# Row flags in one word, the overflow path as one loop, and expert 0's rest without branches

## The chip, the cores and the metric

The kernel runs as one program on one core of a Trainium2 chip. The metric is the device time of one execution in microseconds. Five engines work beside each other, each with its own queue of instructions: TensorE (PE; its weight loads are shown apart as PEld), VectorE (DVE), ScalarE (ACT), GpSimd (POOL) and SyncE (SP). They wait for each other on semaphores. In front of each engine a sequencer takes the program in order: it executes branches, register loads and register arithmetic itself and hands the rest on to the engine. In the profile the sequencers' own rows carry a q (PEldq, SPq, POOLq).

## The reference, cut to what matters

Three stages follow one another: a linear attention, a dense feed-forward layer with a cosine gate, and a layer of 8 experts, of which each token uses one. The change lies between the last two.

```python
logits = x @ w_gate                      # x: 3072 tokens x 384
e_idx = np.argmax(logits, axis=1)
...
for e in range(8):
    mask = e_idx == e
    h = np.maximum(x[mask] @ w1[e], 0.0)     # 384 x 1024
    ye = h @ w2[e]                           # 1024 x 384
    out[mask] = gate_w[mask, None] * eom[mask, e, None] * ye
```

## The kernel before

Attention and the dense layer run interleaved over six groups of 512 tokens. Each token's row is then written by a POOL scatter into the region of its expert in the array `xs`, at a place found by counting (`route_rank`, `route_rows`; `base` holds for each expert its first free row). Each expert has `CAP` = 448 rows that are always computed; what lies above them is done by an overflow path, entered only if an expert has more rows.

An expert's work has two stages. Stage 1 (`e_stage1`) makes the hidden layer in 8 blocks of 128 units (j = 0 to 7): 9 matmuls each, three exact splits times three slices of 128 input dimensions, all rows of the expert at once as columns of one PSUM bank `hp`. ACT then writes the high part of relu(hp), DVE the low part, and only then may PE reuse the bank. Stage 2 (`e_part2`) multiplies each tile of 128 rows of the hidden layer with `w2`; the last, half tile of 64 rows has a form of its own (`e_part2_both`). While one expert runs, the next expert's weights are loaded in 8 pieces through four buffers `raw` (SP), split into a high part (ACT, line 595) and a low part (DVE, line 599), and its rows `xe` are loaded and transposed (`load_rows`, `rows_trans`).

If an expert has at most `LOW` = 384 rows, its `few` flag is set: stage 1 then takes 384 columns instead of 448, and the half tile is left out. Both forms stand in the program, and PE's sequencer branches between them (`by_rows`): once for each of the 8 blocks and once for the half tile, for each expert.

Expert 0 is special. Its first 256 rows (`early`) are done while the dense layer's last group still runs (`first`, `second`); its remaining 192 rows (128 where `few` is set) come after, with the same weights. In the run shown they have 192 columns.

The order on PE, ACT, DVE and SP around this seam is the order in which the code is written (a manual schedule up to the last `second`, program order behind). At the seam the kernel before does this: transposes of expert 0's remaining rows, `second(7)`, start of the load of expert 1's rows, then on DVE the overflow counts `nt` and the flags `few` (lines 1017 to 1030), then on PE a load of 8 flags from SBUF into 8 registers (line 1031), then on DVE the zeroing of three PSUM banks (line 1037), then stage 1 of expert 0's remaining rows on two banks, in turn. In the trace the 8 flags are one TENSOR_LOAD and, for each flag, a FUSED_REGOPS and a SEQ_ASSERT. `ps_m` is a PSUM pool of three banks that the transposes use; at this point of the program it is otherwise free.

At the end every engine loads `nov`, the largest overflow count, and branches around the overflow path, which is written out for 8 experts. In this run it is not entered.

Of the kernel before, what the change touches and what calls it, by code (L numbers as in the profile page):

```python
# [28 lines left out]
E = 8  # L29
# [5 lines left out]
CAP = 448  # L35
# [15 lines left out]
CEB = CW8 + GU * E  # L51
CTOK = CEB + E
CROW = CTOK + NU
CCOL = CROW + 1


@with_exitstack
def kernel(
# [590 lines left out]
    def by_rows(few, sizes):  # L649

        if few is None:
            yield sizes[0]
            return
        with tc.If(few > 0) as cmp:  # L654
            yield sizes[1]
        with cmp.Else():
            yield sizes[0]

    def e_stage1(r, j, hh, hl):
        h1, l1 = ew[r["e"]][:2]  # L660
        xh, xl = r["x"]
        n = r["n"]
        hp = (r["banks"][j % 2] if "banks" in r else ps_h.tile([128, 512], F32, tag="h", name="hp"))[:, :n]
        fs = slice(j * 128, (j + 1) * 128)
        m_n = n - CAP + LOW
        few = r.get("few")
        for m in by_rows(few, (n, m_n)):
            i = 0
            for w, x in ((h1, xh), (h1, xl), (l1, xh)):
                for k in range(KD):  # L670
                    nc.tensor.matmul(  # L671
                        out=hp[:, :m], lhsT=w[:, k, fs], rhs=x[:, k, :m], start=(i == 0), stop=(i == 3 * KD - 1)
                    )
                    i += 1
        nc.scalar.activation(out=hh, in_=hp, func=ACTF.Relu)  # L675
        for c, out_ in hl:
            nc.vector.scalar_tensor_tensor(  # L677
                out=out_, in0=hp[:, c], scalar=0.0, in1=hh[:, c].bitcast(F32), op0=ALU.max, op1=ALU.subtract
            )
        r["h"][j] = (hh, hl[0][1])  # L680
# [264 lines left out]
    with tc.manual_schedule(engines={ENG.PE, ENG.Activation, ENG.DVE, ENG.SP}):  # L945
# [7 lines left out]
        def second(j):  # L953
            for t in range(n_t):
                e_part2(early, t, accs[t], j)
# [22 lines left out]
            x1_rows(g, s)  # L978
        route_rank(g)
        route_rows(g)  # L980
        for s in range(GU):
            route_send(g, s)
        second(1)
# [7 lines left out]
        second(5)  # L991
        first(7)
        second(6)
        m1.close()

        m2 = ExitStack()
# [5 lines left out]
        def begin(e):  # L1002
            r0 = EARLY if e == 0 else 0
            return load_rows(e, r0, CAP - r0, z_p, "xe")
# [4 lines left out]
        for t in range(n_t):  # L1009
# [2 lines left out]


        nt = o_p.tile([128, E + 1], F32, name="nt")
        few = o_p.tile([128, E], F32, name="few", bufs=1)
        fewi = o_p.tile([128, E], U32, name="fewi", bufs=1)
        nc.vector.tensor_tensor(out=nt[:, 0:E], in0=base, in1=ebase, op=ALU.subtract)
        nc.vector.tensor_scalar(
            out=nt[:, 0:E], in0=nt[:, 0:E], scalar1=float(127 - CAP), scalar2=127.0, op0=ALU.add, op1=ALU.max
        )  # L1020
        nc.vector.tensor_reduce(out=nt[:, E:E + 1], in_=nt[:, 0:E], axis=AX.X, op=ALU.max)

        nc.vector.tensor_scalar(
            out=few, in0=base, scalar1=float(LOW), scalar2=None, op0=ALU.subtract
        )
        nc.vector.tensor_tensor(out=few, in0=few, in1=ebase, op=ALU.is_le)
        nc.vector.tensor_copy(ntl, nt)
        nc.vector.tensor_scalar(out=ntl, in0=ntl, scalar1=7, scalar2=None, op0=ALU.logical_shift_right)

        nc.vector.tensor_copy(fewi, few)  # L1030
        few_r = nc.values_load_multi_w_load_instructions(fewi[0:1, 0:E], engines=[ENG.PE], min_val=0, max_val=1)[1]


        banks = [ps_h.tile([128, 512], F32, tag="h", name="hp") for _ in range(2)]
# [2 lines left out]
            nc.vector.memset(b, 0.0)  # L1037

        for e in range(E):
            r["few"], r["banks"] = few_r[e], banks  # L1040
            steps = load_expert(e + 1, vr_p if e % 2 else vl_p) if nxt else []

            def step():
# [37 lines left out]
                e_out(r, t, op, ot)  # L1081
            r = nxt
            nxt = begin(e + 2) if e + 2 < E else None
    m2.close()
    at2.close()


    nov = nc.values_load(ntl[0:1, E:E + 1], min_val=0, max_val=NOV)
    with tc.If(nov > 0):
        with tc.tile_pool(name="ov_p", bufs=1, side="left") as ov_p:  # L1090
            f1 = ov_p.tile([128, KD, EF], F32, name="f1")
            f2 = ov_p.tile([128, NEF, DM], F32, name="f2")
            rid = ov_p.tile([128, 1], F32, name="rid")
            lim = ov_p.tile([128, 1], F32, name="lim")
            far = ov_p.tile([128, 1], F32, name="far")
            ri = ov_p.tile([128, 1], U32, name="ri")
# [4 lines left out]
            oo = ov_p.tile([128, DM], F32, name="oo")  # L1101
            nc.vector.memset(zo, 0.0)
            nc.vector.memset(zo[:, ROW - 1:ROW], float(NT))
            for e in range(E):
                nc.sync.dma_start(out=f1, in_=w1[e].rearrange("(k p) f -> p k f", p=128))
                nc.sync.dma_start(out=f2, in_=w2[e].rearrange("(k p) f -> p k f", p=128))
                r0 = e * REG + CAP
                nc.vector.tensor_scalar_add(rid, c_sb[:, CROW:CROW + 1], float(r0))
                nc.vector.tensor_copy(lim, base[:, e:e + 1])
                n_e = nc.values_load(ntl[0:1, e:e + 1], min_val=0, max_val=NOV)  # L1110
                with tc.For_i(0, n_e, 1) as it:

                    nc.vector.tensor_tensor(out=far, in0=rid, in1=lim, op=ALU.is_lt)
                    nc.vector.scalar_tensor_tensor(
# [5 lines left out]
                        out=xs, out_offset=bass.IndirectOffsetOnAxis(ap=ri, axis=0),  # L1120
                        in_=zo, in_offset=None, bounds_check=E * REG - 1, oob_is_err=False,
                    )
                    nc.sync.dma_start(out=xo[:, 0, :], in_=xs[bass.ds(it * 128 + r0, 128), :])
                    gt, tk = gates(ov_p, xo[:, :, DM:], 1)
                    tp = ps_m.tile([128, KD, C], F32, tag="m", name="tp")
                    for k in range(KD):
# [28 lines left out]
def _layout(inputs):  # L1155
# [32 lines left out]
    for n in range(NU):  # L1188
        c[:, CTOK + n] = (n % B) * S + (n // B) * C + perm
    c[:, CROW] = np.arange(128)  # L1190
    return {
        "units": u.reshape(NU, 128, UCOL),
        "cst": c,
# [26 lines left out]
```

## Time and profile before

| | |
|---|---|
| three timed runs | 814.5 us median, 813.9 to 815.12 |
| the profiled execution | 812.32 us, span 810.5 us, mean granted PE clock 0.981 |
| busy share of the span | PE 95%, DVE 62%, ACT 52%, POOL 39% |
| last transfer into `out` issued at | 800.13 us of the span |

A position in the span is given in us from its start, and so are all times of single instructions. "Granted clock" is the share of 2.4 GHz that TensorE was given; 0.50 is 1.2 GHz. In a row of the timeline the first number is the start, the second the length, "x3" the number of merged instructions, and the bracket tells how long the engine sat idle before and what ended it. The seam lies at 566 to 596 us: in the page's 40 slices PE's tenths are 9 nearly throughout from 140 us on, with one break there.

### The profile page before, as it was taken

How to read it: one execution, taken by the hardware profiler on the slowest of the kernel's cores; microseconds unless marked ns; L12 is line 12 of the kernel's file. 1: busy time of each engine (PE TensorE's matmuls, PEld its weight loads, DVE VectorE, ACT ScalarE, POOL GpSimd, SP SyncE). 2: the span in 40 equal slices, each digit the busy share in tenths (PEclk: the TensorE clock that was granted, in tenths of full speed). 3: DMA queues.
4: the chain of work that ended last, by engine and by line, in shares of the span. 5: the costliest groups of instructions: out<-in, count | busy, mean ns of one | idle time of the engine just before them, and what ended most of it. 6: DMA issues, size and time to landing. Idle time of an engine off the chain costs nothing.

```text
span 810.5 us, 13963 instructions
## 1 busy us (share of the span) xinstructions
PE 769.4 (95%) x5346; PEld 655.7 (81%) x5346; DVE 501.9 (62%) x955; ACT 425.3 (52%) x782; POOL 316.6 (39%) x304
## 2 busy tenths in 40 slices
PE   8679899999999999999999999999699999999994
PEld 5557777888888888888888888889699999999994
DVE  8999998675467537663676334744565655655530
ACT  2454565754575457644665467555354545554420
POOL 3566756544355335543464424662011101101101
PEclk9998999999999999999999999999899999999998
DMA  9524452713201230113010101211565445645201
GB/s 326 205 94 159 170 199 100 243 60 112 80 1 54 73 125 1 54 59 109 31 55 20 41 0 59 89 50 44 182 192 181 135 142 176 191 123 159 67 13 34
DMA packets 46881, 85.31 MB, mean 105 GB/s; under 512 B 4152, under 2 KB 38488, under 8 KB 44240
## 3 DMA queue, kind: packets, MB, share of 16 engines
q1 hardware_dynamic: 43344, 74.67, 28.1%
q0 software_dynamic: 3456, 9.57, 3.2%
q8 instruction: 50, 0.82, 0.4%
q14 instruction: 31, 0.25, 0.1%
HBM read 69.01 MB, written 15.99 MB: 105 GB/s over the span
## 4 chain that ended last, share of the span: by engine, by line
PE 52%; issue 27%; DVE 11%; POOL 4%; DMA 2%; ACT 1%; POOLq 0%; SPq 0%; ACTq 0%; DVEq 0%
PE acc L418 22%; PE hp L379 21%; POOL out_dram L711 4%; DVE cv L347 3%; PE sc L211 2%; DMA un<-in_units_dram 2%; DVE cv L352 2%; PE yp L269 2%; PE yp L261 2%; DVE cv L356 2%; PE pp L285 1%; PE tp L442 1%; DVE t L397 1%; DVE t L392 1%; DVE w L151 1%
## 5 line engine op out<-in xcount | busy, mean ns | idle before, releaser
L405 POOL TENSOR_TENSOR gl<-t,gh 128x512 fp32r<-128x512 f32 x95 | 127.8, 1345 | 182.2 <-ACT gh L404 152.5
L386 ACT ACTIVATE t<-hp 128x512 f32<-128x512 f32 x96 | 57.3, 596 | 140.1 <-PE hp L379 130.4
L397 DVE TENSOR_TENSOR t<-hp,t 128x512 f32<-128x512 f32 x96 | 65.7, 684 | 89.3 <-ACT t L394 89.3
L392 DVE SCALAR_TENSOR_TENSOR t<-t,hp 128x512 f32<-128x512 f32 x96 | 65.7, 684 | 79.7 <-ACT t L386 79.6
L711 POOL DMA_INDIRECT out_dram<-ot,tk x32 | 31.3, 979 | 205.9 <-ACT ot L710 205.6
L687 PE MATMUL op<-h,hb 128*128 128x384 f32 x384 | 102.4, 338 | 1.7 <-PEq L654 1.7
L418 PE MATMUL acc<-gh,woh 128*128 128x512 f32 x288 | 90.3, 421 | 0.0
L677 DVE SCALAR_TENSOR_TENSOR hb<-hp,hb 128x64 fp32r<-128x64 f32 (+3 forms) x136 | 45.3, 372 | 70.1 <-ACT hb L675 70.0
L379 PE MATMUL hp<-xh,wih 128*128 128x512 f32 x288 | 83.6, 398 | 3.7 <-DVE t L397 3.1
L418 PE MATMUL acc<-gl,woh 128*128 128x512 f32 x288 | 84.2, 399 | 0.0
L418 PE MATMUL acc<-gh,wol 128*128 128x512 f32 x288 | 83.9, 399 | 0.0
L379 PE MATMUL hp<-xh,wil 128*128 128x512 f32 x288 | 82.6, 395 | 0.0
L379 PE MATMUL hp<-xl,wih 128*128 128x512 f32 x288 | 82.5, 395 | 0.0
L393 ACT ACTIVATE t<-t 128x512 f32<-128x512 f32 x96 | 60.7, 632 | 38.3 <-DVE t L392 38.3
L675 ACT ACTIVATE hb<-hp 128x448 fp32r<-128x448 f32 (+2 forms) x72 | 36.3, 504 | 72.3 <-PE hp L671 70.3
L599 DVE TENSOR_TENSOR l<-raw,h 128x768 fp32r<-128x768 f32 x60 | 57.3, 957 | 25.8 <-ACT h L595 25.0
L687 PEld LDWEIGHTS op<-h,hb 128*128 128x128 f32 x384 | 69.7, 188 | 3.0 <-issue 3.0
L394 ACT ACTIVATE t<-t,halfpi 128x512 f32<-128x512 f32 x96 | 69.6, 725 | 3.1
L379 PEld LDWEIGHTS hp<-xh,wih 128*128 128x128 f32 x288 | 54.4, 191 | 18.0 <-DVE t L397 2.2
L418 PEld LDWEIGHTS acc<-gh,wol 128*128 128x128 f32 x288 | 55.1, 191 | 13.4
L418 PEld LDWEIGHTS acc<-gl,woh 128*128 128x128 f32 x288 | 54.9, 191 | 12.8
L379 PEld LDWEIGHTS hp<-xl,wih 128*128 128x128 f32 x288 | 54.5, 189 | 12.9
(144 smaller groups left out, 1454.4 us busy)
## 6 DMA issues: line engine op xcount, KB each, us to landing
raw<-in_w_dram SPq DMA_DIRECT2D x64, 384.0 KB, 3.4
un<-in_units_dram SPq DMA_DIRECT2D x20, 1032.0 KB, 4.9
raw<-in_w_in_dram SPq DMA_DIRECT2D x16, 384.0 KB, 3.7
raw<-in_w_out_dram SPq DMA_DIRECT2D x16, 384.0 KB, 4.1
xs<-zrow SPq DMA_DIRECT2D x8, 591.0 KB, 5.8
xe<-xs SPq DMA_DIRECT2D x7, 591.0 KB, 5.1
un<-in_units_dram SPq DMA_DIRECT2D x4, 512.0 KB, 6.2
un<-in_units_dram SPq DMA_DIRECT2D x4, 256.0 KB, 6.8
```

The lines of the kernel that those rows point to most:

```text
L379: nc.tensor.matmul(out=hp, lhsT=w[:, k, fs], rhs=x[:, k, :], start=(n == 0), stop=(n == 3 * KD - 1))
L386: nc.scalar.activation(out=t, in_=hps[g, j], func=ACTF.Copy, bias=MAGIC)
L392: nc.vector.scalar_tensor_tensor(out=t, in0=t, scalar=MAGIC, in1=hp, op0=ALU.subtract, op1=ALU.subtract)
L393: nc.scalar.activation(out=t, in_=t, func=ACTF.Abs)
L394: nc.scalar.activation(out=t, in_=t, func=ACTF.Sin, scale=-TWO_PI, bias=halfpi)
L397: nc.vector.tensor_tensor(out=t, in0=hps.pop((g, j)), in1=t, op=ALU.mult)
L405: eng.tensor_tensor(out=gl, in0=gf, in1=gh.bitcast(F32), op=ALU.subtract)
L418: nc.tensor.matmul(out=acc[g][k], lhsT=w[:, j, ks], rhs=a, start=(j == 0 and n == 0), stop=(j == NF - 1 and n == 2),)
L599: (nc.vector.tensor_tensor if i < 4 else sub)(out=lo, in0=raws[i], in1=h.bitcast(F32), op=ALU.subtract)
L677: nc.vector.scalar_tensor_tensor(out=out_, in0=hp[:, c], scalar=0.0, in1=hh[:, c].bitcast(F32), op0=ALU.max, op1=ALU.subtract)
L687: nc.tensor.matmul(out=op, lhsT=a[:, sl], rhs=w[:, j, :], start=(j == 0 and i == 0), stop=(j == NEF - 1 and i == 2))
L711: sent = nc.gpsimd.indirect_dma_start(out=out, out_offset=bass.IndirectOffsetOnAxis(ap=tk[0:n, t, :], axis=0), in_=ot[0:n], in_offset=None ...
```

## The change

Three edits come together.

1. The flags become bits of one word. Right after the last `route_rows`, DVE computes for each expert whether its count is at most 384, times 2 to the power of the expert's number (a new row of constants), sums the 8 values and converts the sum (four small instructions). PE loads that one word before the transposes of expert 0's remaining rows. Each branch of experts 0 to 7 then tests a bit, with register arithmetic ahead of it. The three DVE instructions and the load of 8 registers at the seam go.
2. Stage 1 of expert 0's remaining rows always takes all 192 columns, with no branch, and goes over three banks in turn: the two of before and one from `ps_m`.
3. The overflow path becomes one loop over the experts instead of 8 copies, and `nov` is loaded before expert 7 instead of at the end.

```diff
-        hp = (r["banks"][j % 2] if "banks" in r else ps_h.tile([128, 512], F32, tag="h", name="hp"))[:, :n]
+        hp = (r["banks"][j % 3 if r["e"] == 0 else j % 2] if "banks" in r and (j % 3 < 2 or r["e"] > 0) else ps_m.tile(
+            [128, 512], F32, tag="m", name="hp") if "banks" in r else ps_h.tile([128, 512], F32, tag="h", name="hp"))[:, :n]
...
-        for m in by_rows(few, (n, m_n)):
+        for m in by_rows(few if r["e"] else None, (n, m_n)):
...
         route_rows(g)
+        cnt = s_p.tile([128, E], F32, tag="rk", name="cnt")
+        nc.vector.tensor_tensor(out=cnt, in0=base, in1=ebase, op=ALU.subtract)
+        nc.vector.scalar_tensor_tensor(
+            out=cnt, in0=cnt, scalar=float(LOW), in1=c_sb[:, CPW:CPW + E], op0=ALU.is_le, op1=ALU.mult
+        )
+        bits = s_p.tile([128, 1], F32, tag="pf", name="bits")
+        nc.vector.tensor_reduce(out=bits, in_=cnt, axis=AX.X, op=ALU.add)
+        fews = s_p.tile([128, 1], U32, tag="pu", name="fews")
+        nc.vector.tensor_copy(fews, bits)
         for s in range(GU):
             route_send(g, s)
...
         second(6)
+        few = nc.values_load(fews[0:1, 0:1], engines=[ENG.PE], min_val=0, max_val=(1 << E) - 1)
...
-        nc.vector.tensor_scalar(
-            out=few, in0=base, scalar1=float(LOW), scalar2=None, op0=ALU.subtract
-        )
-        nc.vector.tensor_tensor(out=few, in0=few, in1=ebase, op=ALU.is_le)
...
-        nc.vector.tensor_copy(fewi, few)
-        few_r = nc.values_load_multi_w_load_instructions(fewi[0:1, 0:E], engines=[ENG.PE], min_val=0, max_val=1)[1]
...
-            r["few"], r["banks"] = few_r[e], banks
+            r["few"], r["banks"] = nc.tensor.snap((few >> e) & 1), banks
...
+            if e == E - 2:
+                nov = nc.values_load(ntl[0:1, E:E + 1], min_val=0, max_val=NOV)
...
-    nov = nc.values_load(ntl[0:1, E:E + 1], min_val=0, max_val=NOV)
-    with tc.If(nov > 0):
+    with tc.If(nov > 0, label="ov"):
...
-            for e in range(E):
-                nc.sync.dma_start(out=f1, in_=w1[e].rearrange("(k p) f -> p k f", p=128))
-                nc.sync.dma_start(out=f2, in_=w2[e].rearrange("(k p) f -> p k f", p=128))
...
+            with tc.For_i(0, E, 1) as e:
+                nc.sync.dma_start(out=f1, in_=w1[bass.ds(e, 1)].rearrange("o (k p) f -> p (o k) f", p=128))
+                nc.sync.dma_start(out=f2, in_=w2[bass.ds(e, 1)].rearrange("o (k p) f -> p (o k) f", p=128))
```

How the seam's instructions stand in the program, for PE and DVE. In PE's order before, from the last matmul of `second(7)` (`op`) over the load of the flags to the first block of stage 1 in its two forms (`hp_5980` is the first bank, `exh`, `exl` the rows, `h1`, `l1` the weights; 128x128 is the few form):

```order
L687 MATMUL op_5687<-h2_5168,hb_5816 128x384
L1031 TENSOR_LOAD fewi_5898 [waits DVE_49,PE_49,Pool_49]
L1031 ISA x16
L654 COMPARE_AND_BRANCH
L671 MATMUL hp_5980<-exh_5859,h1_5166 128x128 [waits DVE_49,Activation_49]
L671 MATMUL hp_5980<-exh_5859,h1_5166 128x128 [waits Activation_49] x2
L671 MATMUL hp_5980<-exl_5860,h1_5166 128x128 x3
L671 MATMUL hp_5980<-exh_5859,l1_5167 128x128 x3
L654 UNCONDITIONAL_BRANCH
L671 MATMUL hp_5980<-exh_5859,h1_5166 128x192 [waits DVE_49,Activation_49]
L671 MATMUL hp_5980<-exh_5859,h1_5166 128x192 [waits Activation_49] x2
```

In PE's order now the load stands earlier, between the last matmul of `second(6)` and the transposes `tp` of expert 0's remaining rows:

```order
L689 MATMUL op_5687<-h2_5168,hb_5804 128x384
L1006 TENSOR_LOAD fews_5736 [waits DVE_49]
L1006 ISA x2
L643 MATMUL tp_5878<-c_sb_112,xe_5872 128x128 [waits DMAHW5_49,PE_49]
L643 MATMUL tp_5878<-c_sb_112,xe_5872 128x128 [waits DMAHW6_49,DVE_49]
```

and behind the last matmul of `second(7)` stage 1 follows at once (its blocks 0 to 2, on three banks `hp_5919`, `hp_5920`, `hp_5966`):

```order
L689 MATMUL op_5687<-h2_5168,hb_5823 128x384
L673 MATMUL hp_5919<-exh_5876,h1_5166 128x192 [waits DVE_49,Activation_49]
L673 MATMUL hp_5919<-exh_5876,h1_5166 128x192 [waits Activation_49] x2
L673 MATMUL hp_5919<-exl_5877,h1_5166 128x192 x3
L673 MATMUL hp_5919<-exh_5876,l1_5167 128x192 x3
L673 MATMUL hp_5920<-exh_5876,h1_5166 128x192 [waits DVE_49]
...
L673 MATMUL hp_5966<-exh_5876,h1_5166 128x192 [waits PE_49]
```

The load with 16 further instructions and the branch have gone from between the two matmuls; the first block still waits for DVE, and the second waits for DVE once more, on its own.

On DVE at the same place, before (from the padding of expert 1's rows `xe` to the zeroing of the banks `hp`, `hp`, `op`):

```order
L630 MEMSET xe_5892 64x394
L1017 TENSOR_TENSOR nt_5896<-base_117,c_sb_112 128x8
L1018 TENSOR_SCALAR nt_5896<-nt_5896 128x8 [waits DVE_49]
L1021 TENSOR_REDUCE nt_5896<-nt_5896 128x1 [waits DVE_49]
L1023 TENSOR_SCALAR few_5897<-base_117 128x8
L1026 TENSOR_TENSOR few_5897<-few_5897,c_sb_112 128x8 [waits DVE_49]
L1027 CAST ntl_118<-nt_5896 128x9
L1028 TENSOR_SCALAR ntl_118<-ntl_118 128x9 [waits DVE_49]
L1030 CAST fewi_5898<-few_5897 128x8
L1037 MEMSET hp_5980 128x512
L1037 MEMSET hp_5981 128x512
L1037 MEMSET op_5982 128x512 [waits Activation_49]
```

and now:

```order
L631 MEMSET xe_5909 64x394
L1028 TENSOR_TENSOR nt_5913<-base_117,c_sb_112 128x8
L1029 TENSOR_SCALAR nt_5913<-nt_5913 128x8 [waits DVE_49]
L1032 TENSOR_REDUCE nt_5913<-nt_5913 128x1 [waits DVE_49]
L1033 CAST ntl_118<-nt_5913 128x9 [waits DVE_49]
L1034 TENSOR_SCALAR ntl_118<-ntl_118 128x9 [waits DVE_49]
L1040 MEMSET hp_5919 128x512
L1040 MEMSET hp_5920 128x512
L1040 MEMSET op_5921 128x512 [waits Activation_49]
```

Three of eight small instructions ahead of the zeroing have gone; the cast of the counts now stands right behind the reduction that it waits for.

In the branches of experts 1 to 7 two instructions of register arithmetic now stand ahead of each compare (one of them in the branch of expert 0's half tile); PE's order now, where expert 1's second block begins:

```order
L655 UNCONDITIONAL_BRANCH
L655 REGISTER_ALU x2
L655 COMPARE_AND_BRANCH
L673 MATMUL hp<-exh,h_5927 128x384 [waits DVE_49,Activation_49]
L673 MATMUL hp<-exh,h_5927 128x384 x2
```

## Rows read from the trace of the kernel before

**Rows 1.** Waits of PE, 575 to 811 us: total us, times, longest.
```profile
PE hp L671 <- issue: 5.4, 1, 5.4
PE op L687 <- PEq L654: 1.7, 4, 0.4
```

**Rows 2.** Timeline at the seam, PE and DVE (columns as told above).
```profile
570.36 0.34 PE L687 MATMUL op<-h,hb 128*128 128x384 f32 x1
...
571.48 0.16 DVE L1023 TENSOR_SCALAR few<-base 128x8 f32<-128x8 f32 x1
...
572.17 0.16 DVE L1030 CAST fewi<-few 128x8 uint32<-128x8 f32 x1
572.44 1.03 DVE L1037 MEMSET hp<- 128x512 f32 x2
...
576.10 0.92 PE L671 MATMUL hp<-exh,h 128*128 128x192 f32 x3 [5.40 <-issue]
```

**Rows 3.** PE's sequencer by source line: ns min/median/max, first to last start.
```profile
L1031 PEldq FUSED_REGOPS  x8: 146/146/160, 573.4 to 575.4; - x8
...
L1031 PEldq TENSOR_LOAD <-fewi x1: 788/788/788, 572.5 to 572.5; - x1
...
L654 PEldq COMPARE_BRANCH  x9: 202/208/337, 575.7 to 586.3; - x9
...
L654 PEldq COMPARE_BRANCH  x4: 207/208/212, 776.1 to 781.8; - x4
...
L1088 PEldq TENSOR_LOAD <-ntl x1: 332/332/332, 795.9 to 795.9; - x1
```

**Rows 4.** Stretches: length, busy of PE PEld DVE ACT POOL, clock, DMA, GB/s.
```profile
570.70:576.07 5.37, 0.00 (x1) 0.00 (x0) 2.94 (x12) 0.62 (x2) 1.99 (x2) 0.91 0.97 306
576.07:581.94 5.87, 5.84 (x27) 5.87 (x28) 1.44 (x5) 1.38 (x3) 0.00 (x0) 0.50 0.18 69
581.94:587.67 5.73, 5.36 (x46) 5.12 (x45) 4.14 (x13) 3.10 (x7) 0.00 (x0) 1.00 0.43 133
587.67:596.03 8.36, 8.36 (x55) 8.32 (x54) 6.06 (x16) 6.25 (x13) 0.92 (x1) 1.00 0.75 228
```

**Rows 5.** Timeline: DVE after the routing, PE at two other places.
```profile
561.20 0.42 DVE L677 SCALAR_TENSOR_TENSOR hb<-hp,hb 128x256 fp32r<-128x256 f32 x1 [2.79 <-ACT hb L675]
...
568.43 0.30 PE L642 MATMUL tp<-c_sb,xe 128*128 128x128 f32 x1 [0.36 <-DMA xe<-xs]
...
783.76 0.34 PE L695 MATMUL op<-h,hb 128*128 128x384 f32 x1
```

**Rows 6.** Timeline: PE at the start of stage 1's block 6.
```profile
585.70 0.55 PE L671 MATMUL hp<-exh,h 128*128 128x192 f32 x3 [0.37 <-ACT hb L675]
```

**Rows 7.** Earlier gaps of PE on the timeline; stretches behind them (columns as rows 4).
```profile
81.92 1.16 PE L211 MATMUL sc<-un 64*128 64x128 f32 x14 [1.40 <-DVE scan L149]
...
136.95 0.96 PE L379 MATMUL hp<-xh,wih 128*128 128x512 f32 x3 [1.80 <-DVE t L397]
...
82.00:89.00 7.00, 6.98 (x32) 5.33 (x32) 6.97 (x11) 2.18 (x5) 4.68 (x3) 0.76 0.31 105
87.00:94.00 7.00, 5.55 (x27) 4.33 (x26) 6.96 (x15) 3.72 (x7) 4.29 (x5) 1.00 0.59 213
137.00:143.00 6.00, 6.00 (x19) 4.76 (x20) 2.78 (x5) 4.64 (x9) 5.31 (x8) 0.72 0.60 199
```

**Rows 8.** Source line 588, 566 to 575 us: SP's loads of weights, ns, starts, landing.
```profile
L588 SPq DMA_DIRECT2D raw<-in_w_dram x4: 421/451/516, 568.1 to 569.8; - x4
...
DMA to landing us min/median/max: 5.3/6.5/7.3
```

**Rows 9.** POOL's sequencer at the end (lines 1089, 711): branch, next events, landing.
```profile
L1089 POOLq EVENT_SEMAPHORE  x5: 17/43/43, 803.3 to 803.7; - x5
...
L1089 POOLq COMPARE_BRANCH  x1: 53/53/53, 800.4 to 800.4; - x1
...
DMA to landing us min/median/max: 3.0/3.0/3.0
```

More of the change, by code (lines that the diff above doesn't have):

```diff
@@ L53 @@
 CROW = CTOK + NU
-CCOL = CROW + 1
+CPW = CROW + 1
+CCOL = CPW + 16
 @with_exitstack
@@ L1014 @@
         nt = o_p.tile([128, E + 1], F32, name="nt")
-        few = o_p.tile([128, E], F32, name="few", bufs=1)
-        fewi = o_p.tile([128, E], U32, name="fewi", bufs=1)
         nc.vector.tensor_tensor(out=nt[:, 0:E], in0=base, in1=ebase, op=ALU.subtract)
@@ L1093 @@
             rid = ov_p.tile([128, 1], F32, name="rid")
+            rs = ov_p.tile([128, 1], F32, name="rs")
+            ends_ = ov_p.tile([128, E], F32, name="ends_")
+            next_ = ov_p.tile([128, E], F32, name="next_")
             lim = ov_p.tile([128, 1], F32, name="lim")
@@ L1103 @@
             nc.vector.memset(zo[:, ROW - 1:ROW], float(NT))
-            for e in range(E):
-                nc.sync.dma_start(out=f1, in_=w1[e].rearrange("(k p) f -> p k f", p=128))
-                nc.sync.dma_start(out=f2, in_=w2[e].rearrange("(k p) f -> p k f", p=128))
[L1107 to L1111, printed above, removed]
+            nc.vector.tensor_scalar_add(rs, c_sb[:, CROW:CROW + 1], float(CAP))
+            nc.vector.tensor_copy(ends_, base)
+            with tc.For_i(0, E, 1) as e:
+                nc.sync.dma_start(out=f1, in_=w1[bass.ds(e, 1)].rearrange("o (k p) f -> p (o k) f", p=128))
+                nc.sync.dma_start(out=f2, in_=w2[bass.ds(e, 1)].rearrange("o (k p) f -> p (o k) f", p=128))
+                nc.vector.tensor_copy(rid, rs)
+                nc.vector.tensor_scalar_add(rs, rs, float(REG))
+                nc.vector.tensor_copy(lim, ends_[:, 0:1])
+                nc.vector.tensor_copy(next_, ends_)
+                nc.vector.tensor_copy(ends_[:, 0:E - 1], next_[:, 1:E])
+                with tc.For_i(0, nov, 1) as it:
                     nc.vector.tensor_tensor(out=far, in0=rid, in1=lim, op=ALU.is_lt)
@@ L1122 @@
                     )
-                    nc.sync.dma_start(out=xo[:, 0, :], in_=xs[bass.ds(it * 128 + r0, 128), :])
+                    nc.sync.dma_start(out=xo[:, 0, :], in_=xs[bass.ds(it * 128 + e * REG + CAP, 128), :])
                     gt, tk = gates(ov_p, xo[:, :, DM:], 1)
@@ L1190, in _layout @@
     c[:, CROW] = np.arange(128)
+    c[:, CPW:CPW + E] = 2.0 ** np.arange(E)
     return {
```

## Prediction

> **What bounds the kernel now.** The page's busy shares come first: PE is busy for 95% of the span, so time is lost or won where PE stands still or runs slowly. The view of PE's waits over the expert part is read next. It has one large entry, 5.4 us in one piece before stage 1 of expert 0's remaining rows; the only other above half a microsecond is four times 0.4 us at branches [rows 1]. So the seam is where a change of this kind can act. The timeline there shows what the 5.4 us consist of [rows 2]: PE's last matmul ends at 570.70, the flags are ready on DVE at 572.33, the first two banks are zeroed from 572.44 to 573.47, and PE starts at 576.10. DVE therefore explains less than half of it. The rest stands in the rows of PE's sequencer, which the timeline of the engine doesn't show [rows 3]: a TENSOR_LOAD of 0.79 us from 572.5, eight rounds of register work from 573.4 to 575.55, and then the first branch at 575.7. "Issue" as the reason for the wait is this sequencer work.
>
> The stretches show the second cost [rows 4]. Behind the gap the granted clock is 0.50 for 5.87 us and PE needs that time for 27 matmuls; at the full clock the next 45 take 5.73 us, small holes included. Stage 1 as a whole lasts 576.07 to 587.67, 11.60 us. The rest of expert 0, half tile, transposes and full tile, lasts 8.36 us with PE busy throughout, so there is nothing to win there.
>
> **The change part by part.** *The wait at the seam.* The load of the flags and its 16 further instructions leave this place, and so do three DVE instructions of about 0.16 us [rows 2]. Late next is the zeroing of the first bank, which DVE reaches only behind the counts `nt`. Without the three instructions it starts about 0.4 us before 572.44 (0.5 less, 0.1 given back because the cast now stands right behind the reduction that it waits for). One bank is half of 1.03 us, so it is ready at about 572.55, and with 0.15 us for the semaphore PE starts at 572.7. The gap is then 2.0 instead of 5.4 us: −3.4. The bounds: 572.6, if the semaphore is quicker, and 573.6, if the first matmul should have to wait for all three banks (two more of 0.5 us each); I take the early end, since the new order has a DVE wait of its own on the second block.
>
> *The load in its new place* costs PE's sequencer one TENSOR_LOAD and one round of register work: between 0.33 us (the load of a single word) and 0.79 us (the load of eight), plus 0.3 [rows 3]. Behind it in PE's queue stand the transposes, and for these ACT, DVE and `second(7)` wait. Two things hide it. The sequencer is ahead of the engine: near the end its last branch of stage 1 runs at 781.8, while PE begins what stands behind that branch at 783.76 [rows 3, 5], nearly 2 us later, and the single-word load at 795.9 leaves no hole in PE. And PE waits 0.36 us for the transposes' rows there anyway [rows 5]. I take nothing; without that cover it is at most 1.1 us. The four new DVE instructions fall into DVE's idle time of 2.79 us before 561.20 [rows 5]: nothing.
>
> *Stage 1.* Blocks 6 and 7 run at full clock from 585.70 [rows 6] to 587.67, one microsecond each. Eight such blocks are 8.1 us with a little room, against 11.60: 3.5 less. Of this 5.87 / 2 = 2.9 is the low clock, and 0.6 the waits for a bank (0.37 before block 6 [rows 6]) and the small holes at branches. Three banks let PE run one block further ahead of ACT and DVE; expert 0's flag is not set in this run, its blocks have 192 columns before as well, so the missing few form costs nothing. DVE is near its limit here (4.14 us busy of 5.73 in the second half [rows 4]), so up to 0.6 us of the bank waits may stay.
>
> *The clock.* The 3.4 and the 0.6 us are safe; the 2.9 hang on whether a gap of 2.0 us still lowers the clock. Rows on both sides [rows 7]: a gap of 1.80 us ended at 136.95, and in the 6 us from 137 the mean clock is 0.72, which is 3.4 us at 0.50. A gap of 1.40 us ended at 81.92, and the mean of the next 7 us is 0.76, again 3.4 us at 0.50. But from 87 to 94 PE is idle for 1.45 us and the clock stays at 1.00. Two of three shorter gaps did lower it, so I take it that the clock falls, for 3.4 us instead of the 5.87: half of it, 1.7 us, is lost.
>
> *The loads of expert 1* are late next. Its first four pieces are issued from 568.1 to 569.8 and land 5.3 to 7.3 us later, by 577.1 [rows 8]; stage 1 uses them from about 575 on, one per two blocks. The other four wait for a buffer that DVE frees, and that moves with stage 1. From 576.07 to 596.03 DVE is busy for 1.44 + 4.14 + 6.06 = 11.6 us and ACT for 10.7 [rows 4]; the new stretch is 8.1 + 8.4 = 16.5 us plus the low clock. Both fit, so expert 1 starts early by the whole sum. From there on every expert has the work of before.
>
> *Register arithmetic at the branches* of experts 1 to 7: two instructions of 0.146 us with their dispatch, 0.3 us, for each of 63 branches. The sequencer's lead of nearly 2 us covers it: nothing (the rival below has the other end).
>
> *The end.* The loads of `nov` move ahead of expert 7 on four engines but POOL; 0.33 us on PE's sequencer under that lead. POOL's branch at 800.4 is followed by its next event only at 803.3 [rows 9], 2.9 us later; the last scatter, issued at 800.13, lands 3.0 us after its issue. If the shorter overflow path made the jump cheap, POOL would still wait until 803.1: at most 0.2 us, and I take 0. The Trainium skill, "Runtime: NRT & Kernel Launch", section "Instruction fetch mechanics", says that a taken branch to a target outside the instructions at hand stalls for a fetch of that target; by it the 2.9 us are such a fetch and the shorter path would give the 0.2. For the branches of expert 0, which were taken to the wide form, the rows speak against it: they last 0.20 to 0.34 us [rows 3].
>
> *The sum:* −3.4 − 2.9 − 0.6 + 1.7 = −5.2. The profiled execution took 812.3 (span 810.5 and 1.8 around it); this gives 807.1. The timed runs' median is 814.5, 2.2 above the profiled one, and I carry the difference over: **809.3**.
>
> **The rivals.**
> *The clock holds.* All as above, without the 1.7: −6.9, 807.6. For it: 1.45 us idle and no fall [rows 7]. Against it: 1.80 us with one.
> *The clock falls for as long as before.* 2.9 instead of 1.7 are lost: −4.0, 810.5. It needs a second slow stretch although PE is busy from 572.7 on; after the two shorter gaps there was none.
> *The gain is given back at expert 1.* If weights or rows of expert 1 came no earlier, PE would wait at its first blocks. DMA moves 306 GB/s in the gap itself [rows 4], so these loads have competition. Price: up to all but a half microsecond, 814. Against it: the four first pieces have landed by 577.1, and DMA is at a share of 0.18 thereafter.
> *Slower: the branches come to the path.* The place is PE's sequencer in stage 1 of experts 1 to 7. If its lead were used up there, 63 × 0.3 = 19 us would be added, 828 in all. It decides from 0.08 us shown per branch on, since 63 × 0.08 are the 5.2 us of gain. Against it: a block takes 1.6 to 1.9 us, the branch 0.2 with 0.3 new, and 72 branches leave only four holes, at the jumps over the half tile [rows 1].
> *It doesn't do what it says:* if the first matmul waits for all three banks and the load is uncovered, the gap is 2.9 us and 1.1 come on top; −3.4 + 0.9 + 1.1 − 0.6 with the clock as before, −2.0: 812.5.
>
> **How the numbers follow.** The forecast has 0.48, the clock that holds 0.24, the long low clock 0.08, the late banks and load 0.07, the gain given back 0.07, the slower branches 0.06. The forecast alone spans 808 to 810.5. The range goes from 806.2 (a clock that holds, with the 0.2 of the end and a microsecond for the timing) to 812.0 (the long low clock with the 1.1 of the load, rounded up); outside stay the gain given back, the slower branches and a part of the late banks. What a measurement of this kernel can tell from no change is 0.2%, 1.6 us: faster is all below 812.9, and that is the first four cases, 0.87; the gain given back makes 0.07 for no difference; slower has 0.06.
>
> **What would show it.** PE's gap before stage 1 should be about 2 us, ended by DVE's zeroing and not by issue; a gap that stays near 5 us proves the first step wrong. The stretch behind it should show a clock of 0.50 for about 3.4 us, or 1.00 throughout (first rival). Stage 1's eight blocks should follow without waits for ACT, in 8 to 10 us. Expert 1's first block should start some 5 us earlier than 596.03, and the distance from there to the last scatter should be the old 204.1 us; more there means branches or loads. The forecast is wrong if the time is above 812 or if the gain shows up in another place than the seam.

## The result, and the profile after

The changed kernel takes 804.36 us (median of 4 runs, 803.06 to 806.81), the kernel before 814.71 in the same sitting: a ratio of 0.9878 [0.9851, 0.9904], 10.35 us less. A second sitting gave 0.9895 [0.9881, 0.9909]. The forecast was 809.3 with a range down to 806.2: right in sign, wrong in size, and the time lies below the range. The profiled execution of the changed kernel took 805.11 us, with a span of 803.3; its trace is read first.

The seam is as forecast. The first fence has PE's waits from 571 to 804 us, to be set beside [rows 1]; the second the timeline at the seam [rows 2].

```profile
PE hp L673 <- DVE hp L1040: 2.3, 1, 2.3
PE op L689 <- PEq L655: 1.8, 4, 0.5
```

```profile
571.96 0.34 PE L689 MATMUL op<-h,hb 128*128 128x384 f32 x1
...
573.21 0.45 DVE L1033 CAST ntl<-nt 128x9 uint32<-128x9 f32 x1
573.70 0.17 DVE L1034 TENSOR_SCALAR ntl<-ntl 128x9 uint32<-128x9 uint32 x1
573.98 1.02 DVE L1040 MEMSET hp<- 128x512 f32 x2
...
574.61 0.83 PE L673 MATMUL hp<-exh,h 128*128 128x192 f32 x3 [2.31 <-DVE hp L1040]
```

The gap of 5.40 us that ended by "issue" is one of 2.31 that ends by DVE's zeroing: PE's sequencer is out of it, and what is late next is the counts and the first zeroed bank. The four holes at the jumps over the half tile are what they were. In the sequencer's own rows (compare [rows 3]) the load stands ahead of the transposes, and the register arithmetic of experts 1 to 7 is cheaper than assumed, 0.036 us an instruction and not 0.146:

```profile
L1006 PEldq TENSOR_LOAD <-fews x1: 483/483/483, 566.9 to 566.9; - x1
L1006 PEldq FUSED_REGOPS  x1: 165/165/165, 567.5 to 567.5; - x1
...
L655 PEldq ALU_OP  x127: 36/36/42, 583.2 to 777.5; - x127
```

The stretches have the columns of [rows 4], the first two with PE's busy time alone: the gap, stage 1, and from expert 1's first block to the last scatter; in the second fence the last of these in the kernel before.

```profile
572.30:574.61 2.31, 0.00 (x0) 1.00 0.99 308
574.61:584.34 9.73, 9.73 (x73) 0.82 0.52 159
...
592.66:795.71 203.05, 200.29 (x1129) 192.72 (x1128) 106.29 (x228) 95.39 (x173) 27.45 (x28) 1.00 0.43 131
```

```profile
596.03:800.13 204.10, 201.47 (x1129) 192.97 (x1128) 106.21 (x228) 95.40 (x173) 27.44 (x29) 1.00 0.42 130
```

Stage 1 has no wait left. A mean clock of 0.82 over 9.73 us is 2 × 0.18 × 9.73 = 3.5 us at half clock (0.50, the level of 1.2 GHz), which costs half of that. But two things stand in places where the forecast had none: the 203 us of the other experts are 1.05 us shorter, and so is the end. POOL's sequencer there, after and then before (compare [rows 9]; ns min/median/max, first to last start):

```profile
L1093 POOLq COMPARE_BRANCH  x1: 45/45/45, 796.0 to 796.0; - x1
L1093 POOLq EVENT_SEMAPHORE  x1: 17/17/17, 796.5 to 796.5; - x1
L1093 POOLq INC_SWDGE_SEM  x1: 1278/1278/1278, 796.6 to 796.6; - x1
...
L1228 POOLq DRAIN  x3: 45/107/4638, 797.9 to 803.1; - x3
```

```profile
L1089 POOLq INC_SWDGE_SEM  x1: 1286/1286/1286, 803.8 to 803.8; - x1
...
L1216 POOLq DRAIN  x3: 40/107/4647, 805.1 to 810.3; - x3
```

POOL goes from its branch to its next event in 0.5 us instead of 2.9, and does not wait for the scatter issued at 795.71, whose data land some 2.9 us later. What ends the span is its queue: branch, INC_SWDGE_SEM of 1.3 us, DRAIN of 4.6 us.

The whole span of both traces, cut at the same events:

| stretch, us | before | after | difference | forecast |
|---|---|---|---|---|
| start to the end of `second(7)` on PE | 570.70 | 572.30 | +1.60 | 0 |
| gap | 5.40 | 2.31 | −3.09 | −3.4 |
| stage 1 | 11.66 | 9.73 | −1.93 | −1.8 |
| rest of expert 0 | 8.27 | 8.32 | +0.05 | 0 |
| expert 1 to the issue of the last scatter | 204.10 | 203.05 | −1.05 | 0 |
| that issue to the end | 10.37 | 7.59 | −2.78 | 0 |
| sum | 810.50 | 803.30 | −7.20 | −5.2 |

### The profile page after: what moved, and what is told of

Its sections match the earlier page's. It is cut to its first block, busy times and chain, and to the rows that moved or that the text cites. A ratio compares the mean times of both kernels' runs of the same rounds, so it can differ in the third digit from the quotient of the medians.

```text
span 803.3 us, 14056 instructions
## 1 busy us (share of the span) xinstructions
PE 766.4 (95%) x5346; PEld 653.3 (81%) x5346; DVE 502.4 (63%) x956; ACT 425.2 (53%) x782; POOL 317.2 (39%) x304
## 4 chain that ended last, share of the span: by engine, by line
PE 53%; issue 26%; DVE 11%; POOL 5%; DMA 2%; ACT 1%; POOLq 0%; SPq 0%; DVEq 0%; ACTq 0%
PE acc L419 22%; PE hp L380 21%; POOL out_dram L713 4%; DVE cv L348 3%; PE sc L212 2%; DVE cv L353 2%; PE yp L270 2%; PE yp L262 2%; DVE cv L357 1%; PE pp L286 1%; DMA un<-in_units_dram 1%; PE tp L443 1%; DVE w L152 1%; DVE t L393 1%; DVE t L398 1%
```

## The experiments

**The three edits apart.** Four kernels, each with its own comparison with the kernel before. The first is the kernel before with only the new general path, its count loaded at the end as ever:

```diff
-            for e in range(E):
+            with tc.For_i(0, E, 1) as e:
...
-                with tc.For_i(0, n_e, 1) as it:
+                with tc.For_i(0, nov, 1) as it:
```

> The kernel before with one edit: the general path as one loop, its count still loaded at the end. Theory (the end waits for code): the path from the last scatter's issue to the end runs through POOL's branch, its INC_SWDGE_SEM (1.3 us) and its DRAIN (4.6 us), and with the short path the 2.9 us between POOL's branch and its next instruction become 0.5. The stretch from the last scatter's issue to the end of the span goes from 10.4 to 7.6 us, and the time falls by 2.8 us (ratio 0.9966); nothing else moves. Rival (the recorded prediction): the end waits for the landing of the last scatter, and the time falls by 0 to 0.2 us (ratio 0.9998 to 1).

Measured: 810.03 us, ratio 0.9956 [0.9943, 0.997], 3.4 us less; the interval holds the 2.8. The trace has 7.6 us from the last scatter (802.58) to the end, and POOL's sequencer reads

```profile
L1089 POOLq COMPARE_BRANCH  x1: 45/45/45, 802.9 to 802.9; - x1
L1089 POOLq EVENT_SEMAPHORE  x1: 17/17/17, 803.4 to 803.4; - x1
L1089 POOLq INC_SWDGE_SEM  x1: 1296/1296/1296, 803.4 to 803.4; - x1
```

The loop alone does it, without the early load of the count. The recorded step "at most 0.2" falls.

The opposite: the changed kernel with the eight copies back.

```diff
-            with tc.For_i(0, E, 1) as e:
+            for e in range(E):
...
+    nov = nc.values_load(ntl[0:1, E:E + 1], min_val=0, max_val=NOV)
```

> The changed kernel with the general path written out eight times again and its count loaded at the end: the flags as one word and stage 1 of expert 0 on three banks stay. Theory (the end waits for code): the end takes 10.4 us again, so the time is 2.8 us over the changed kernel's, some 7.5 us under the kernel before (ratio 0.9908). Rival (the recorded prediction): the end doesn't matter, and the whole gain of 10.3 us stays (ratio 0.9875).

Measured: 805.93 us, ratio 0.9904 [0.9888, 0.9919]: the theory's 0.9908 lies in the interval, the rival's 0.9875 below it. Its end takes 10.2 us in the trace. That this end costs 2.6 us more than the changed kernel's rests on the traces; set beside that kernel's two ratios, 0.9878 and 0.9895, the times show 0.7 to 2.1 us.

Next, the changed kernel with the branches and two banks back in expert 0, so with the early word and the loop alone:

```diff
-        hp = (r["banks"][j % 3 if r["e"] == 0 else j % 2] if "banks" in r and (j % 3 < 2 or r["e"] > 0) else ps_m.tile(
...
+        hp = (r["banks"][j % 2] if "banks" in r else ps_h.tile([128, 512], F32, tag="h", name="hp"))[:, :n]
-        for m in by_rows(few if r["e"] else None, (n, m_n)):
+        for m in by_rows(few, (n, m_n)):
```

> The changed kernel with stage 1 of expert 0 as before: a branch in each of its eight steps, two banks in turn. Theory (three separate gains): the gap ahead of stage 1 is 2.3 us as in the changed kernel, ended by the zeroing of the banks or by the first branch, at most 3; stage 1 itself takes 11 to 11.6 us instead of 9.7, so the time is 1.5 to 2.5 us over the changed kernel's (ratio to the kernel before 0.990 to 0.992). Rival (the branches are hidden once the word is early, and the clock sets stage 1 alone): stage 1 takes 9.7 us and the time equals the changed kernel's within 0.5 us. Rival (branches after the early load stall as the one at the end did): over 3 us more.

And the kernel before with the three banks alone, the same lines the other way round:

> The kernel before with one edit: stage 1 of expert 0 on three banks without branches; the eight flags are still loaded by PE at the seam. Theory (PE's queue is in order, so the load of eight registers holds stage 1 back although nothing in it reads them): the gap ahead of stage 1 stays at 4.5 to 5.4 us, stage 1 falls from 11.6 to 9.0 to 9.8 us, and the time falls by 2 to 3 us (ratio 0.9963 to 0.9975). Rival (the first branch was what cost the gap): the gap falls to 2 to 2.6 us, and the time falls by 5 us (ratio 0.994).

Measured: 804.63 us for the first, 0.9891 [0.9876, 0.9906], and 812.33 for the second, 0.9991 [0.9982, 1.0]. PE in the gap and in stage 1, first without the three banks, then with them alone:

```profile
571.00:573.31 2.31, 0.00 (x1) 1.00 1.02 275
573.31:583.80 10.49, 10.15 (x73) 0.84 0.62 207
```

```profile
570.98:576.53 5.55, 0.00 (x1) 0.87 1.06 329
576.53:587.18 10.65, 10.65 (x72) 0.75 0.24 70
```

With the early word the gap is 2.31 us although the branches are there; with the eight flags loaded at the seam it is 5.55 us although no branch of expert 0 reads them. So the gap belongs to the load in PE's in-order queue, not to the branch. Three banks without branches take 0.8 us out of stage 1 in the trace (10.49 to 9.73 at about the same low clock, banks and branches not parted). In the times this step is too small: 0.9891 without it, 0.9878 and 0.9895 with it. Both expectations were 1 to 2 us too high here. So by the time the rival (equal within 0.5 us) is not ruled out, and the 0.8 us rest on the traces. The sizes add up: the early word is worth 5.4 us (810.03 to 804.63; in the traces 1.05 of it comes with experts 1 to 7, see below), the loop 3.4, the banks alone 0.7 (by the ratio) to 1.1 (by the medians); together 9.5 to 9.9 of the 10.35.

**The gap and the clock.** Of four kernels in one sitting the first is the changed kernel unaltered.

> The changed kernel unaltered, as the other half of each comparison and as a second trace of it. The stretch ahead of stage 1, its length in the clock's two levels and the end are to be as in the first trace: a gap of 2.3 us, an end of 7.6 us. Theory (the clock at the seam differs from run to run): the low stretch there may be 0 or 3.4 us, and the ratio to the kernel before stays at 0.985 to 0.990. Rival (the first trace is what every run does): 3.4 us low again, and the times agree within 0.5 us.

Measured: 804.73 us; gap 2.32, stage 1 9.72 us at a mean clock of 0.82, so again 3.5 us low. This trace alone speaks for the rival; but the kernel with eight copies above and the one with four below have the same gap, word and banks, and no fall at all. Here is the latter:

```profile
572.44:574.75 2.31, 0.01 (x1) 1.00 1.03 282
574.75:582.84 8.09, 8.09 (x72) 1.00 0.67 217
```

In seven traces with a gap of 2.3 us the clock fell in four and held in three. Stage 1 takes 8.1 us where it holds and 9.7 where it falls. Neither branch of the forecast was wrong; they take turns. The three that held are those in which `second(7)` ended latest, at 572.36 to 572.75 us of the span against 569.72 to 572.30. Seven traces are too few to call that a cause, so what decides stays open.

The second kernel zeroes the two hp banks earlier in DVE's order, in its idle time ahead of the transposes:

```diff
+        banks = [ps_h.tile([128, 512], F32, tag="h", name="hp") for _ in range(2)]
+        for b in banks:
+            nc.vector.memset(b, 0.0)
         rows_trans(r, z_p, "exh", "exl")
         second(7)
```

> The changed kernel with the zeroing of the two hp banks moved up in VectorE's order, ahead of the last chunk's transposes, where VectorE idles 1.7 us. Theory (the gap is VectorE's: rows, counts, then zeroing): the gap of 2.3 us falls to 0.2 to 0.6, the clock holds at the seam, and the time falls by 1.9 us, by 2 to 3.6 us where the clock had fallen (801 to 802.5 us). Rival (PE then waits for something else, the weights or exl, as long): the gap stays over 1.5 us and the time moves by less than 0.8 us. Rival (zeroing delays exl by 1 us): the gap falls by 1 us at most.

Measured: **800.23 us**, ratio 0.9838 [0.9825, 0.9851], 4.5 us under the changed kernel. Its seam and its stage 1:

```profile
569.66 1.03 DVE L1022 MEMSET hp<- 128x512 f32 x2
...
571.80 0.34 PE L689 MATMUL op<-h,hb 128*128 128x384 f32 x1
...
571.98 0.48 PE L673 MATMUL hp<-exh,h 128*128 128x192 f32 x3
```

```profile
571.98:580.00 8.02, 8.02 (x74) 1.00 0.97 297
```

No gap, no fall of the clock, stage 1 in 8.0 us: the seam is closed, and this kernel beats both. The expectation was too low: 2.3 us of gap and 1.7 of clock are 4.0 of the 4.5 measured.

The third lengthens the gap by work on DVE alone, and the fourth keeps PE busy in it:

```diff
+        for _ in range(5):
+            nc.vector.memset(banks[0], 0.0)
```

```diff
+        idle = ps_m.tile([128, 512], F32, tag="m", name="idle")
+        for _ in range(18):
+            nc.tensor.matmul(out=idle, lhsT=ew[0][0][:, 0, 0:128], rhs=ew[0][0][:, 0, 0:512], start=True, stop=True)
```

> The changed kernel with five more zeroings of the first hp bank ahead of the three that stand there: VectorE takes 2.5 us more, so the gap ahead of stage 1 is 4.8 us, nearly that of the kernel before (5.4). Nothing else is changed. Theory (the gap's price is its length and, beyond that, the low clock that follows it): the low stretch is 6.8 us instead of 0 to 3.4, and the time rises by 2.5 us for the gap and 1.7 to 3.4 us for the clock, together 4.2 to 5.9. Rival (the gap's length alone counts): 2.5 us.

> The kernel with the longer gap, and 18 matmuls of 512 columns put into it whose result nobody reads: PE works for some 4 us of the 4.8 us while VectorE zeroes. Theory (the clock falls because PE idles): no low stretch at the seam, stage 1 in 8.1 us; the time lies 1.7 to 3.4 us under the kernel with the idle gap and 2.5 us over the changed kernel at most. Rival (the clock falls for another reason, as for the transposes or the small matmuls ahead): the low stretch stays and the two kernels agree within 0.5 us.

Measured: 808.77 and 806.93 us, ratios 0.9945 [0.9926, 0.9965] and 0.9925 [0.9906, 0.9944]. The first, then the second:

```profile
570.41:576.05 5.64, 0.00 (x1) 0.97 1.01 340
576.05:587.22 11.17, 11.16 (x72) 0.71 0.17 44
```

```profile
571.04:575.32 4.28, 4.28 (x19) 1.00 1.05 310
575.32:576.85 1.53, 0.00 (x1) 1.00 1.07 397
576.85:586.58 9.73, 9.73 (x73) 0.82 0.27 70
```

A gap of 5.64 us made by DVE brings back 6.8 us of low clock (0.03 × 2 × 5.64 + 0.29 × 2 × 11.17) and from the end of `second(7)` to expert 1 the 25.1 us of the kernel before (25.3), without any of its flags or branches. That stretch is 4.8 us longer than in the changed kernel (20.3): 3.3 of gap, 1.4 of stage 1. The median is 4.0 us over the changed kernel's in this sitting, just under the expected 4.2 to 5.9 and well over the rival's 2.5. With PE busy for 4.28 of the 5.8 us the low clock is 3.5 us, half as long; none of the eight traces with 5.4 us or more of idle has less than 6.7. From the end of `second(7)` to expert 1 it takes 23.7 us instead of 25.1. The medians differ by 1.8 us, but the two intervals overlap, so the times alone don't show it. The traces say that the low clock follows PE's idle time; the expectation "no low stretch" was wrong: 1.53 us of idle were left, and behind them the clock was low.

**How far the branch jumps.** The loop's body written out twice, and four times:

```diff
-            with tc.For_i(0, E, 1) as e:
+            with tc.For_i(0, E // 2, 1) as e:
+                for u in range(2):
```

> The changed kernel with the body of the general path's loop written out twice (four trips over two experts each). Theory (the branch at the end waits for code that lies beyond what the engine holds; how far it jumps decides, engine by engine): with twice the code in the loop the engines with the longest path pay first, PE and VectorE 2.9 to 3.3 us after their branch, while POOL, with the shortest, may still pass in 0.5 us; then the end stays at 7.6 us, as PE's and VectorE's branches are done before POOL's. Rival (the loop form itself, or the number of semaphores behind the branch, decides): every engine passes as in the changed kernel, 0.3 to 0.6 us.

> The changed kernel with the body of the general path's loop written out four times (two trips over four experts each). Theory (distance decides): all engines wait about 2.9 us behind the branch, POOL too, and the end takes 10.4 us, as with eight copies; if POOL's path is still short enough, 7.6 us with the others late. Rival (the loop form decides): 7.6 us, and 0.3 to 0.6 us at every engine's branch.

Measured in one execution each: with two copies 802.57 us and an end of 7.7, with four 806.34 and 10.1. The branches, two copies and then four:

```profile
L1093 POOLq EVENT_SEMAPHORE  x2: 17/30/43, 793.9 to 793.9; - x2
...
L1093 PEldq COMPARE_BRANCH  x1: 325/325/325, 788.9 to 788.9; - x1
...
L1093 POOLq COMPARE_BRANCH  x1: 45/45/45, 793.4 to 793.4; - x1
```

```profile
L1093 POOLq EVENT_SEMAPHORE  x4: 17/43/43, 795.1 to 797.5; - x4
L1093 SPq COMPARE_BRANCH  x1: 45/45/45, 750.6 to 750.6; - x1
L1093 DVEq COMPARE_BRANCH  x1: 63/63/63, 781.5 to 781.5; - x1
L1093 DVEq EVENT_SEMAPHORE  x1: 21/21/21, 782.1 to 782.1; - x1
L1093 PEldq COMPARE_BRANCH  x1: 3327/3327/3327, 790.1 to 790.1; - x1
...
L1093 POOLq COMPARE_BRANCH  x1: 45/45/45, 794.7 to 794.7; - x1
```

With two copies every engine still passes, which was the rival's forecast. With four PE's branch takes 3.3 us instead of 0.3, while DVE, which the theory had among the first to pay, still passes in 0.6. So for PE it is the amount of code jumped over that decides, somewhere between two copies and four, and not the loop form. In the Trainium skill, "Runtime: NRT & Kernel Launch", section "Instruction fetch mechanics", a taken branch waits for a fetch where its target is outside the instructions at hand; that agrees with PE's rows (0.3 against 3.3 us). That the hole is a fetch no run shows directly.

POOL's late semaphore is another matter. It passes its first semaphore 0.46 us after its branch but the last only at 797.5. The trace names the semaphore of each instruction: the last one waits for number 118, which the last scatter raises as its data land, and that landing was complete at 797.47. So POOL waits here for the last scatter, and not for its branch. Which semaphores it waits for after the branch depends on the copies (times in us):

| copies | POOL waits for semaphores | first passed, after the branch | last scatter landed at | 118 passed at | issue of the last scatter to the end |
|---|---|---|---|---|---|
| 1 (changed kernel) | 111, 112 | 0.47 | 798.61 | no such wait | 7.6 |
| 2 | 111 to 114 | 0.47 | 796.01 | no such wait | 7.7 |
| 4 | 111 to 118 | 0.46 | 797.47 | 797.50 | 10.1 |
| 8 (kernel before) | 122, 111 to 118 | 2.89 | 803.11 | 803.67 | 10.4 |

So two things kept the kernel before late at its end, and they ran side by side: the hole of 2.9 us behind POOL's branch, and the wait for the last scatter. With four copies the first is gone, and the end gains only 0.3 us; with two copies or one both are gone, and it gains 2.6 to 2.8. For POOL the rival that named the semaphores behind the branch was right. No run has the hole without the wait. The DRAIN that ends the span does not depend on that landing: it takes 4.64 us where the scatter had landed 1.4 us before it began (four copies) and where it landed 0.7 us into it (changed kernel).

**The kernel before, twice more.**

> The kernel before unaltered, for a second trace. Theory (the low clock at the seam lasts 6.8 us in some runs and 10.2 us in others, 1.7 us apart in time): a run of about 814 us has 10.2 us, one of about 812.3 us has 6.8 us; the gap is 5.4 to 6 us and the end 10.4 us in either. Rival (the times of the kernel before differ by something ahead of the seam): 6.8 us again, whatever the time, and the last matmul ahead of the gap ends at another time.

> The kernel before unaltered, a third trace, with the same expectations as the second: about 814 us with 10.2 us of low clock at the seam, or about 812.3 us with 6.8 us; by the rival the difference lies ahead of the seam.

Measured: 812.99 and 814.35 us. Gap and stage 1 of each:

```profile
571.47:577.03 5.56, 0.01 (x1) 0.78 1.01 316
577.03:587.97 10.94, 10.57 (x72) 0.80 0.31 98
```

```profile
572.03:577.77 5.74, 0.00 (x1) 0.69 0.93 317
577.77:589.78 12.01, 11.64 (x72) 0.72 0.21 68
```

By 2 × (1 − clock) × length that is 6.8 and 10.3 us at half clock, and 16.5 against 17.75 us from the end of `second(7)` to the end of stage 1. The two traces agree with the theory; the rest of the 1.4 us is ahead of the seam (+0.6) and at the end (−0.4). But a time of about 814 us doesn't by itself tell the long stretch: the kernel before with 16 idle columns (next) took 813.99 us with 6.7 us of low clock, and there `second(7)` ended only at 572.76, so the rival has a share too.

**Where the 1.05 us of experts 1 to 7 come from.** In the changed kernel three matmuls of 448 columns in expert 6 take 0.60 us from start to start, before 0.62. The word was one candidate; the other was that the 16 new columns of `c_sb` move every tile behind it by 64 bytes. So the kernel before with idle columns, and the changed kernel with more:

```diff
-CCOL = CROW + 1
+CCOL = CROW + 17
```

> The kernel before with 16 idle columns in c_sb, which moves the tiles behind it by 64 bytes as the change does; the flags, the branches and the general path are as before. Theory (the place of the tiles sets the pace of the 448-column matmuls): three of them take 0.60 us, and from the start of expert 1's stage 1 to the issue of the last scatter it takes 203.0 us instead of 204.1. Rival (the early word, one register in place of eight, sets it): 0.62 us and 204.1 us.

> The kernel before with 8 idle columns in c_sb (32 bytes). Theory (place): the pace follows the address, so it may be 0.60 or 0.62, and the stretch 203.0 or 204.1 us with it; whichever it is belongs to every such matmul. Rival (the early word): 0.62 us and 204.1 us.

> The changed kernel with 16 more idle columns in c_sb (128 bytes beside the kernel before). Theory (place): if 64 bytes turn the pace one way, another 64 may turn it back, so 0.62 and 204.1 us, or it stays at 0.60 and 203.0. Rival (the early word): 0.60 us and 203.0 us whatever the place. Alone this run tells little; with the other two it does.

Measured in one execution each: 813.99, 812.02 and 804.43 us. Expert 6 on PE in the kernel before, and in the same with 16 idle columns:

```profile
741.12 0.78 PE L671 MATMUL hp<-exh,h 128*128 128x448 f32 x3
741.74 0.78 PE L671 MATMUL hp<-exl,h 128*128 128x448 f32 x3
```

```profile
741.28 0.76 PE L671 MATMUL hp<-exh,h 128*128 128x448 f32 x3
741.88 0.76 PE L671 MATMUL hp<-exl,h 128*128 128x448 f32 x3
```

0.60 us without the word, 0.62 with 8 idle columns, 0.61 with the word and 16 more. So the pace in expert 6 goes with the place of the tiles and not with the word. The distance from expert 1 to the last scatter is 203.6, 203.7 and 203.9 us in the three, between 203.05 and 204.1: the expected 203.0 was not reached. With 16 idle columns the place alone gives 0.46 us of the 1.05 (stage 1 of experts 1, 6 and 7 is 14.69, 14.40, 14.87 us with 16 idle columns; 14.66, 14.40, 14.59 after; 14.88, 14.87, 14.87 before): expert 6's share is there, expert 7's is not, though with 8 idle columns expert 7 has it (14.59) and expert 6 doesn't (14.88). The changed kernel also drops two tiles of 32 bytes, `few` and `fewi`, so its tiles need not lie where 16 idle columns put them. Where the other 0.6 us come from is not shown; which tile sets the pace, and why, stays open.

## Why the prediction was wrong

*The step that failed* is **The end**: "POOL would still wait until 803.1: at most 0.2 us, and I take 0." In the kernel before that wait is there: POOL passes semaphore 118, the last scatter's, at 803.67, and the kernel with four copies shows that this wait holds the end at 10.05 us, 0.3 less than 10.37. The word that failed is "still": the loop has no such wait. In the changed kernel POOL waits for semaphores 112 and 111 alone, passes the first at 796.51, 2.1 us ahead of the landing at 798.61, and the end is 2.78 us shorter, 2.75 with the loop alone. The prediction carried the wait over without asking which semaphores the changed program waits for, and so put a term of 2.8 us at nothing.

That the hole of 2.9 us is the branch's, as the prediction supposed, other engines' rows in the trace of the kernel before bear out:

```profile
L1089 DVEq EVENT_SEMAPHORE  x2: 21/21/21, 790.8 to 790.9; - x2
...
L1089 DVEq COMPARE_BRANCH  x1: 63/63/63, 787.9 to 787.9; - x1
L1089 PEldq COMPARE_BRANCH  x1: 3304/3304/3304, 796.4 to 796.4; - x1
```

DVE passes its first semaphore 2.9 us after its branch, 9 us before the last scatter is issued; PE's branch itself takes 3.3. The branches of expert 0, whose 0.20 to 0.34 us the prediction held against a stall, jump over one block and say nothing of a long jump.

*The seam was right.* Gap 2.31 against 2.0, ended by DVE; stage 1 9.73 against 9.8; the load hidden; expert 1 not late. From the end of `second(7)` to expert 1 the forecast is 25.3 − 5.2 = 20.1 us, and the traces have 20.4 and 20.3. The bank waits went as forecast, all of them. The clock was the one real choice, and the runs show both: 3.4 us low in four traces of seven. That the profiled run showed the branch chosen is in part luck.

*The register arithmetic* cost nothing, as said; the rival of 828 us falls with 0.036 us an instruction and no new hole. *The branches after the load* likewise.

*The distance of 204.1 us* was called unchanged; it lost 1.05 us, a term the sum did not have; 0.46 of it comes with the place of the tiles alone, the rest is not shown.

*Carrying over 2.2 us* from the profiled run to the median treats the difference as belonging to every kernel. It did not hold here: the changed kernel's profiled runs (805.11, 804.73) lie within 0.8 us of their medians. Two traces of the kernel before have 6.8 us of low clock at the seam and one, at 814.35 us, has 10.3; the changed kernel's two have 3.5. So a part of what makes the kernel before vary sits in the gap that the change shortens; another lies ahead of the seam, where the three traces differ by 1.3 us. That the timed runs have the long stretch is not shown.

*The sum once more*, from 809.3: −2.8 for the end, −1.05 for experts 1 to 7, −2.2 for what was carried over, +0.2 for the seam, and +1.6 since PE's `second(7)` ended later in this trace. That gives 805.05, the profiled run is 805.11. The 1.6 us need not be the change's: in the traces of this case that step ends at 570.7 to 572.8 us without the early word and at 569.7 to 572.8 with it. The range failed for the same reason: its lower end, 806.2, had 0.2 for the end in it; with 2.8 it would be 803.6.

## What to carry to other kernels

Follow the last engine's rows to the end of the span, and ask of each wait which semaphore it is for, in the changed program too: a wait of the kernel before need not be there any more. Code that is never entered can still cost time, by the jump over it (3.3 us on PE from four copies on, 2.9 on POOL over eight) and by the semaphores that are waited for behind it. A wait of PE at a seam has two prices, its length and the low clock behind it; the second differs from run to run, so take two or three traces before you size it. Where a change moves an allocation, compare the pace of the same matmuls elsewhere before you credit the change with what they gain.

## What was not expected of the hardware

- A branch over eight or four copies of the general path takes PE 3.3 us and over two copies 0.3; over four copies DVE passes in 0.6 and POOL in 0.5 us, over eight both take 2.9.
- With four copies or eight POOL waits behind that branch for the landing of the last scatter; with one or two it doesn't.
- After the same idle gap of 2.3 us the granted clock held at 1.00 in three traces and fell to 0.50 for some 3.4 us in four; after 5.4 to 6.1 us it fell for 6.8 us in six traces and for 10.3 in two.
- Tiles moved by 64 bytes change three 448-column matmuls in one expert from 0.62 to 0.60 us with the program otherwise the same; over all seven experts this came to 0.46 us.
- The execution ends 7.6 us after the issue of the last scatter at the earliest seen, 4.6 of them a DRAIN on POOL's queue.
